# A Fourier transform and soft-routed expert kernel on one core: a new written order for the first phase's 404 steps, and seven PSUM banks of one kind

## The chip, the cores and the metric

The kernel runs on one core of one Trainium2 chip. Its time is device time in microseconds (us), from launch to end. It was timed three times before the change: 188.17, 188.81 and 190.61 us, so the median is 188.81 us. The engines are PE (TensorE matmuls; PEld is its weight loads), DVE (VectorE), ACT (ScalarE), POOL (GpSimd) and SP, which here only issues DMAs.

## The reference

```python
X = np.fft.fft(x, axis=1); X = np.fft.fft(X, axis=2)      # x: (8, 2496, 256)
x = X.real.reshape(8 * 2496, 256)
logits = x @ phi                                           # phi: (256, 32)
d = np.exp(logits - logits.max(0)); d /= d.sum(0) + 1e-9   # over all 19968 rows
slot_input = (d.T @ x).reshape(8, 4, 256)
slot_out[e] = np.maximum(slot_input[e] @ w1[e], 0) @ w2[e] # 8 experts, w1 256x1024, w2 1024x256
c = np.exp(logits - logits.max(1)); c /= c.sum(1) + 1e-9   # over the 32 slots
return c @ slot_out.reshape(32, 256)                       # (19968, 256)
```

All of it is float32.

## The kernel before

The eight sequences are handled as four pairs p = 0 to 3. Each pair's rows come in five tiles x (p, t), 1 MB each, with every row next to its mirror row. The transform is never formed in full: it is pushed through phi and through the sums.

**Phase one** is a chain of small steps per pair, named by a letter code, a pair and one or two indices:

- `f`, `g` (lines 254 and 260, DVE): add the second batch row of a tile to the first, then form the even part and the odd part in `eo`. `g` has two steps for each tile, and after both the tile's buffer is free.
- `pt`, `et` (lines 289 and 295): PE transposes `eo` into a PSUM bank, and ACT copies it out. For pair 3 the host already supplies the tile turned round as well (`xT`), so its `h` and `et` (lines 275 and 279) are DVE sums with no PE work, and the plain tiles of pair 3 come later, for `f` and `g` alone.
- `z`, `zs`, `zt`, `ztc`, `a`, `ac`, `lp`, `lm`, `lc`, `l0`, `l1` (lines 310 to 410): matmuls, transposes and copies that end in the logits of the pair, in halves.
- `mx`, `mt`, `ml`, `me`, `mu`, `nm`, `ex`, `dp` (lines 416 to 458): the maximum over a group of rows, its way through PE and back (`me` spreads it with its sign turned, `nm` copies it out of PSUM), the exponential on ACT, and sums and differences of it on DVE.
- `e`, `ec`, `d`, `dc`, `tok`, `tc`, `u`, `uc` (lines 470 to 538): the transform of the weights, copied out of PSUM, and the weighted sum of `eo`. `u` is 40 matmuls, eight for each of the pair's five `eo` tiles.

Each step is a closure, and the list PLAN says in which order they are recorded. PE, DVE and ACT keep that order exactly. An engine waits at a step whose input is not there, with everything behind it.

**Between the phases** (from line 585): `part_m` joins the four pairs, makes the slot inputs `sT`; `part_l` multiplies by w1 (line 644), applies the relu on ACT (652), and transposes on DVE (656); `part_v` multiplies by w2 into the tile `so` (664); `part_r` spreads the result into `rh` (679 to 681).

**Phase two** takes the softmax over the slots (`logits`, `less_max`, `exp`, `over_sum`: cT, cm and c, lines 696 to 723), transposes it (lT, line 757), multiplies by `rh` (po, 779), copies each bank out on ACT or DVE (787) and writes 20.4 MB (792). ORDER lists its parts.

**Loads.** SP issues all of them, in one order. A load waits for its buffer: there are six buffers of 1 MB for x and xT (`ring`), and 15 of 512 KB for `eo`. The weights reuse them. The load w1_0 takes the buffer of the last xT tile, after its two `et` steps; w1_1 to w1_5 take the buffers of pair 3's plain tiles, each after its two `g` steps; w1_6, w1_7 (in halves) and the first w2 piece take pair 1's `eo` after `u1`; the next five w2 pieces pair 2's after `u2`, then five pair 3's after `u3`; the last three wait until `part_l` has read w1 pieces. w1 and w2 are 8.4 MB each. A load that waits holds up all loads behind it.

**PSUM** has eight banks of 512 columns: two of the kind p1 (for pt, z and, later, cT and lT), five of the kind pp (for all else) and one for `u` and `so`. After line 681 the pp banks and the last one become six po banks.

Of the kernel before, what the change touches and what calls it, by code (L numbers as in the profile page):

```python
# [17 lines left out]
GS = 3  # L18
# [12 lines left out]
DE = 2  # L31
FIRST = [0, 1]
GATE = {0: ['u', 'acc', 'acc'], 1: ['rep', 'rep', 'rep']}
P1, P2 = 2, 5
W2 = [1, 1, 1, 1, 1, 1, 1, 1, 1, 1, 1, 2, 2, 1]
PLAN = (
# [97 lines left out]
def _build(nc, tc, xh, xth, phih, w1h, w2h, cins, where, out):  # L134
# [4 lines left out]
    with ctx:  # L139
        cp = ctx.enter_context(tc.tile_pool(name="cp", bufs=1))  # L140
        sb = ctx.enter_context(tc.tile_pool(name="sb", bufs=1))
        p1 = ctx.enter_context(tc.tile_pool(name="p1", bufs=P1, space=PSUM))
# [3 lines left out]
        pool_o = []  # L146
# [19 lines left out]
        def bank1(name, dt=F32):  # L166
            return p1.tile([128, 512], dt, name=name, tag="p1")
# [78 lines left out]
        def x_steps(p, t):  # L246
# [15 lines left out]
            def dest(k):  # L262
                if qi == 0:
                    tr[p, u, k] = et([128, 4, 2, nq, NA], f"et{p}_{u}_{k}")
                return tr[p, u, k][:, :, :, qi]
# [19 lines left out]
            def turn(k):  # L285
                b = held["pt", p, t, k] = bank1(f"pt{p}_{t}_{k}")
                dest(k)
# [50 lines left out]
        def a_steps(p, b):  # L338
# [36 lines left out]
            def _():  # L375
                if b == 0:
                    o1[p] = sa([120, 2, NG, NA], f"o1{p}")
# [496 lines left out]
```

## Time and profile before

| what | us |
| --- | --- |
| median of three timed runs | 188.81 (188.17 to 190.61) |
| the profiled execution, whole | 187.61 |
| its span, first to last instruction | 185.8 |
| PE, DVE, ACT, POOL busy in the span | 159.2, 133.4, 103.3, 20.9 |
| bytes moved | 64.27 MB, 346 GB/s over the span |

The profile is of one execution. A busy PE is not a PE at its peak, because matmuls are pipelined and their ends are modelled; so the rows of PE are read by when one group starts after another. The chain of waits follows the work that ended last back to the start.

### The profile page before, as it was taken

The page shows a single profiled execution, that of the slowest core. Times are in us where ns is not written, and L with a number is a line of the kernel's source. Part 1 is how long each engine was busy: PE and PEld are TensorE (multiplying, and loading weights), DVE is VectorE, ACT ScalarE, POOL GpSimd, SP SyncE. Part 2 cuts the span into 40 slices and gives each one's busy share as a digit, 9 for nine tenths or more (in the row PEclk, how much of TensorE's full clock was granted, in tenths as well). Part 3 has the DMA queues.
Part 4 walks back from the last instruction along what each step waited for, and adds up shares of the span by engine and source line. Part 5 has one row for each costly group of instructions (what it writes and reads, how often), then busy time and mean ns, then how long its engine had stood idle before and what let it go on. Part 6 is the DMA issues. An engine that isn't in the chain of part 4 may idle for free.

```text
span 185.8 us, 4196 instructions
## 1 busy us (share of the span) xinstructions
PE 159.2 (86%) x1674; PEld 101.1 (54%) x1674; DVE 133.4 (72%) x243; ACT 103.3 (56%) x232; POOL 20.9 (11%) x25
## 2 busy tenths in 40 slices
PE   0399858999999999999999999966967998989920
PEld 0384448678757587559759773533534454364410
DVE  0599869959998999999994366700595986892630
ACT  2035563659679486459458434402777797753620
POOL 0000000000000000000000006400055522540000
PEclk9999996999999999999999999999999999955975
DMA  5999999999973099745999999991399999998896
GB/s 167 410 427 414 421 418 418 425 415 424 418 253 164 4 356 363 296 146 185 407 411 356 412 410 406 421 409 70 118 403 412 389 402 424 417 416 351 370 423 284
DMA packets 11394, 64.27 MB, mean 346 GB/s; under 512 B 1392, under 2 KB 1776, under 8 KB 6128
## 3 DMA queue, kind: packets, MB, share of 16 engines
q1 hardware_dynamic: 11376, 64.02, 86.2%
q8 instruction: 13, 0.21, 0.5%
q14 instruction: 5, 0.04, 0.1%
HBM read 43.57 MB, written 20.45 MB: 344 GB/s over the span
## 4 chain that ended last, share of the span: by engine, by line
PE 61%; DMA 25%; DVE 3%; ACT 3%; issue 1%; POOL 1%; SPq 1%; DVEq 0%; ACTq 0%
PE po L779 16%; DMA w<-w2h 13%; DMA x<-xh 12%; PE a L366 6%; PE z L310 6%; PE e L470 5%; PE d L492 5%; PE pt L289 5%; PE u L527 4%; PE lT L757 3%; PE lm L395 3%; PE lp L395 3%; PE zt L349 2%; ACT o L787 1%; DVE x L254 1%
## 5 line engine op out<-in xcount | busy, mean ns | idle before, releaser
L779 PE MATMUL po<-lTs,rh 32*128 32x512 f32 (+2 forms) x192 | 34.0, 617 | 2.5 <-ACT lTs L760 2.5
L787 DVE COPY o<-po 128x512 f32<-128x512 f32 (+1 forms) x40 | 25.1, 665 | 11.7 <-PE po L779 11.6
L254 DVE TENSOR_TENSOR x<-x 128x1024 f32<-128x1024 f32 (+1 forms) x20 | 23.3, 1165 | 9.6 <-DMA x<-xh 9.6
L289 PE MATMUL pt<-cs,eo 128*128 128x128 f32 x120 | 20.2, 308 | 10.5 <-DVE eo L260 10.3
L295 ACT COPY et<-pt 128x512 f32<-128x512 f32 x30 | 17.3, 594 | 19.0 <-PE pt L289 18.7
L787 ACT COPY o<-po 128x512 f32<-128x512 f32 (+1 forms) x40 | 21.3, 581 | 9.7 <-PE po L779 9.3
L260 DVE TENSOR_TENSOR eo<-x 128x512 f32<-128x512 f32 x40 | 25.7, 684 | 0.4
L289 PEld LDWEIGHTS pt<-cs,eo 128*128 128x128 f32 x120 | 15.4, 158 | 15.4 <-DVE eo L260 7.7
L779 PEld LDWEIGHTS po<-lTs,rh 32*128 32x128 f32 x192 | 14.7, 209 | 14.0 <-ACT lTs L760 5.9
L310 PE MATMUL z<-et,wphi 128*32 128x256 f32 (+1 forms) x288 | 17.5, 363 | 0.8 <-ACT et L295 0.7
L713 POOL TENSOR_TENSOR c<-c,cm 128x640 f32<-128x640 f32 x8 | 10.0, 1263 | 64.4 <-DVE cm L712 64.4
L451 ACT ACTIVATE d<-lt,nm 120x128 f32<-120x128 f32 x44 | 13.7, 392 | 0.2 <-DVE nm L444 0.2
L366 PE MATMUL a<-cs,zt 128*120 128x128 f32 x88 | 12.3, 292 | 0.0
L366 PEld LDWEIGHTS a<-cs,zt 128*120 128x120 f32 x88 | 11.0, 196 | 1.4 <-issue 1.4
L723 POOL TENSOR_TENSOR c<-c,cm 128x640 f32<-128x640 f32 x8 | 10.1, 1264 | 11.6 <-DVE cm L722 11.1
L310 PEld LDWEIGHTS z<-et,wphi 128*32 128x32 f32 x288 | 7.4, 112 | 7.1 <-ACT et L295 2.0
L492 PE MATMUL d<-e,cs 128*64 128x320 f32 x64 | 11.1, 448 | 0.0
L470 PE MATMUL e<-cs,dpm 120*64 120x120 f32 x176 | 10.4, 269 | 0.0
L527 PE MATMUL u<-eo,ds 128*32 128x129 f32 x320 | 10.3, 274 | 0.0
L664 PE MATMUL so<-w,hT 128*32 128x256 f32 x128 | 7.7, 381 | 3.0 <-DMA w<-w2h 3.0
L470 PEld LDWEIGHTS e<-cs,dpm 120*64 120x64 f32 x176 | 9.1, 137 | 1.9 <-issue 0.4
L716 ACT ACTIVATE c<-c 128x640 f32<-128x640 f32 x8 | 5.9, 739 | 6.5 <-POOL c L713 6.5
(90 smaller groups left out, 214.5 us busy)
## 6 DMA issues: line engine op xcount, KB each, us to landing
x<-xh SPq DMA_DIRECT2D x16, 1024.0 KB, 12.0
out<-o SPq DMA_DIRECT2D x13, 1024.0 KB, 5.3
w<-w1h SPq DMA_DIRECT2D x6, 1024.0 KB, 7.3
w<-w2h SPq DMA_DIRECT2D x12, 512.0 KB, 11.2
xT<-xth SPq DMA_DIRECT2D x4, 1024.0 KB, 10.5
x<-xh SPq DMA_DIRECT2D x4, 896.0 KB, 9.4
out<-o SPq DMA_DIRECT2D x4, 896.0 KB, 6.0
out<-o SPq DMA_DIRECT2D x5, 512.0 KB, 3.7
```

Source lines behind the costliest of these rows:

```text
L254: v.tensor_tensor(x[:, first:4], x[:, first:4], x[:, 4 : 8 - first], op=ALU.add)
L260: v.tensor_tensor(eo[p, t][:, :, 128 * k : 128 * k + 128], lo, hi, op=(ALU.add, ALU.subtract)[k])
L289: pe.transpose(b[:, g * 128 : g * 128 + 128], eo[p, t][:, g, k * 128 : k * 128 + 128], ident)
L295: sc.copy(tr[p, u, k][:, :, :, qi], b.rearrange("p (g h a) -> p g h a", g=4, h=2))
L310: pe.matmul(z[32 * g : 32 * g + 32, o : o + n], wphi[:, w, :], tr[p, u, k][:, g].rearrange("p h q a -> p (h q a)"), start=w != 0, stop=w != 1,
L366: pe.matmul(ps[:120, i * 128 : i * 128 + 128], zt[p][:, GS * g : GS * g + GS].rearrange("p s h c -> p (s h c)"), C("wa"), start=True, stop ...
L451: sc.activation(d[:, g], L()[:, g], AF.Exp, bias=nm[:, g : g + 1], scale=1.0)
L470: pe.matmul(ps[64 * k : 64 * k + 64, 120 * i : 120 * i + 120], dpm[p, hf][:, k, 3 * j + i, :], C(name), start=True, stop=True, tile_positi ...
L492: pe.matmul(ps[64 * h : 64 * h + 64, :320], C("wb")[:, 64 * k : 64 * k + 64], esb[p].rearrange("p g (s h c) -> p (g s) h c", h=2, c=NKC)[: ...
L527: last = pe.matmul(ub[32 * g : 32 * g + 32, 0:129], dsb[p][:, k, c, :], e[:, 0:129] if k == 0 else e[:, 127:256], start=cc == 0, stop=cc == 9,
L779: ins = pe.matmul(po[h][:, q * n : q * n + n], rh[0][rows, dc], lT[rows, :n], start=True, stop=True, tile_position=(32 * i, 0),)
L787: ins = ev(ot[:, at_ : at_ + w], po[h][:, :w])
```

## The change

PLAN is a different order of the same 404 steps. ORDER is the same. A list ON_V names the steps of kinds `et`, `ac`, `ec`, `dc`, `nm` and `me` that DVE does; the others of these kinds are on ACT. Before, DVE did all eight `me`, all eight `nm` and the eight `dc` of odd index. Now it does two `nm`, two `dc`, two `et` and five `ec`, eleven steps in all.

The pool p1 is opened only after line 681. Until then pt, z, cT and lT take banks of pp, which has seven. The step that makes a tile first is no longer always index 0, so tests of the kind `b == 0` become tests of whether the tile is there. In GATE the third cT of pair 0 is held until the slot inputs instead of the joined sum.

```diff
-DE = 2
-GATE = {0: ['u', 'acc', 'acc'], 1: ['rep', 'rep', 'rep']}
-P1, P2 = 2, 5
+GATE = {0: ['u', 'acc', 'slot'], 1: ['rep', 'rep', 'rep']}
+P1, P2 = 2, 7
 PLAN = (
-    "f00 g001 g000 pt001 pt000 et001 f01 psphi et000 g011 g010 pt011 f02 pt010 et011 wphi g021 z001 et010 "
...
+    "f00 g001 g000 pt001 pt000 et001 f01 psphi g011 g010 pt011 f02 et011 wphi g021 et000 z001 g020 f03 pt010 "
...
+ON_V = (
+    "et031 et100 nm30 ec211 ec210 dc200 nm31 ec301 ec310 ec311 dc310"
+).split()
...
-        p1 = ctx.enter_context(tc.tile_pool(name="p1", bufs=P1, space=PSUM))
-        pool_o = []
+        pool_o, p1 = [], []
...
-            return p1.tile([128, 512], dt, name=name, tag="p1")
+            return p1[0].tile([128, 512], dt, name=name, tag="p1") if p1 else bank(name, dt)
+
+        def move(key, dst, src):
+            (v.tensor_copy if key in ON_V else sc.copy)(dst, src)
...
-                sc.copy(tr[p, u, k][:, :, :, qi], b.rearrange("p (g h a) -> p g h a", g=4, h=2))
+                move(f"et{p}{t}{k}", dest(k), b.rearrange("p (g h a) -> p g h a", g=4, h=2))
...
-                v.tensor_scalar(mex, m.unsqueeze(2).to_broadcast([n, GS, 40]), -1.0, None, op0=ALU.mult)
+                src = m.unsqueeze(2).to_broadcast([n, GS, 40])
+                if "me" + q in ON_V:
+                    v.tensor_scalar(mex, src, -1.0, None, op0=ALU.mult)
+                else:
+                    sc.mul(mex, src, -1.0)
...
-                v.tensor_copy(nm, held.pop(("mt", q))[:120, 128 : 128 + n])
+                move("nm" + q, nm, held.pop(("mt", q))[:120, 128 : 128 + n])
...
-                    sc.copy(esb[p][:, a0 : a0 + w, :].rearrange("p g n -> p (g n)"), ps[:, : 120 * w])
+                    move(f"ec{q}{j}", esb[p][:, a0 : a0 + w, :].rearrange("p g n -> p (g n)"), ps[:, : 120 * w])
...
-                    (v.tensor_copy if DE >> k & 1 else sc.copy)(dst, ps[:, :320].rearrange("p (s c) -> p c s", c=NKC))
+                    move(f"dc{q}{k}", dst, ps[:, :320].rearrange("p (s c) -> p c s", c=NKC))
...
             banks.close()
+            p1.append(ctx.enter_context(tc.tile_pool(name="p1", bufs=P1, space=PSUM)))
```

**Place one: DVE ahead of the loads w1_1 to w1_4.** In these names `eo3_1<-x3_1` is a `g` step of pair 3, tile 1; `x3_0<-x3_0` is its `f`; `dpm` is `dp`, `lt` is `l1` or `l0`, `mex` is `me`. Before:

```order
L444 COPY nm2_0_1011<-mt2_0_964 120x6
L254 TENSOR_TENSOR x3_0_125<-x3_0_125 128x768
L502 COPY ds1_947<-d1_1_1_1008 128x20x16
L444 COPY nm2_1_1035<-mt2_1_975 120x5
L260 TENSOR_TENSOR eo3_0_1037<-x3_0_125 128x4x128 x2
L457 TENSOR_TENSOR dpm2_0_1052<-d2_0_1017 120x384
L458 TENSOR_TENSOR dpm2_0_1052<-d2_0_1017 120x384
L260 TENSOR_TENSOR eo3_1_1098<-x3_1_127 128x4x128 x2
L260 TENSOR_TENSOR eo3_2_1107<-x3_2_129 128x4x128 x2
```

And now:

```order
L264 TENSOR_TENSOR eo3_1_965<-x3_1_124 128x4x128
L419 TENSOR_REDUCE mx2_1_975<-lt2_736 120x5
L264 TENSOR_TENSOR eo3_1_965<-x3_1_124 128x4x128
L264 TENSOR_TENSOR eo3_3_993<-x3_3_128 128x4x128
L430 TENSOR_REDUCE mall_99<-mt2_1_987 5x3
L464 TENSOR_TENSOR dpm1_1_1001<-d1_1_958 120x320
L465 TENSOR_TENSOR dpm1_1_1001<-d1_1_958 120x320
L264 TENSOR_TENSOR eo3_4_1012<-x3_4_130 128x4x128
L409 TENSOR_TENSOR lt3_1006<-lt3_1006,lm3_0_999 120x6x64
L264 TENSOR_TENSOR eo3_4_1012<-x3_4_130 128x4x128
```

Tile 0 of pair 3 was first and is now last of the five; the first load in this series waits for tile 1, the second for tile 4, then 3, 2 and 0. The `nm` and `dc` of pairs 1 and 2 are gone from this engine's row.

**Place two: PE around the arrival of tile (1, 2).** `pt1_2_1` needs that tile, `a0_0` only pair 0. Before:

```order
L349 MATMUL zt0_2_320<-cs0_70,zs0_215 128x128 x2
L289 MATMUL pt1_2_1_325<-cs0_70,eo1_2_311 128x128 x4
L289 MATMUL pt1_1_0_333<-cs0_70,eo1_1_273 128x128 x4
L366 MATMUL a0_0_340<-cs2_72,zt0_266 120x128 x4
L289 MATMUL pt1_2_0_346<-cs0_70,eo1_2_311 128x128 x4
L310 MATMUL z1_0_356<-et1_0_1_288,wphi_100 32x256 x8
```

And now:

```order
L369 MATMUL a0_2_319<-cs2_69,zt0_283 120x128 x3
L369 MATMUL a0_1_323<-cs2_69,zt0_283 120x128 x4
L369 MATMUL a0_0_329<-cs2_69,zt0_283 120x128 x4
L292 MATMUL pt1_1_0_337<-cs0_67,eo1_1_299 128x128 x4
L398 MATMUL lp0_1_345<-o10_334,cs2_69 120x320
L398 MATMUL lm0_1_349<-o10_334,cs2_69 120x320
L292 MATMUL pt1_2_0_352<-cs0_67,eo1_2_342 128x128 x4
```

The three `a` of pair 0 and half of its `lp` and `lm` now stand ahead of the first transpose that needs tile (1, 2).

**Place three: DVE after the slot inputs.** `cm0` and `c0` are pair 0's softmax, `hT` the transposed hidden layer. Before:

```order
L626 COPY sT_1370<-slotin1_1441 128x32
L712 TENSOR_REDUCE cm0_0_1494<-c0_1476 128x20
L712 TENSOR_REDUCE cm0_1_1502<-c0_1476 128x20
L720 TENSOR_REDUCE cm0_0_1494<-c0_1476 128x20
L721 TENSOR_SCALAR cm0_0_1494<-cm0_0_1494 128x20
L722 RECIPROCAL cm0_0_1494<-cm0_0_1494 128x20
```

And now:

```order
L633 COPY sT_1367<-slotin1_1438 128x32
L663 STREAM_TRANSPOSE hT00_1458<-hs00_1456 128x512
L663 STREAM_TRANSPOSE hT01_1471<-hs01_1469 128x512
L720 TENSOR_REDUCE cm0_0_1491<-c0_1473 128x20
L720 TENSOR_REDUCE cm0_1_1499<-c0_1473 128x20
L663 STREAM_TRANSPOSE hT10_1518<-hs10_1516 128x512
```

The hidden layer's transposes came after the whole of pair 0's softmax and now go among it.

## Rows read from the trace of the kernel before

**Rows 1.** The page's slices: GB/s moved in 40 equal slices of the span.

```profile
GB/s 167 410 427 414 421 418 418 425 415 424 418 253 164 4 356 363 296 146 185 407 411 356 412 410 406 421 409 70 118 403 412 389 402 424 417 416 351 370 423 284
```

**Rows 2.** Stretches: length, busy PE, PEld, DVE, ACT, POOL, clock, DMA share, GB/s.

```profile
28.50:40.00 11.50, 11.44 (x119) 8.82 (x120) 10.04 (x13) 6.38 (x12) 0.00 (x0) 0.85 1.01 422
80.00:97.00 17.00, 16.94 (x212) 11.26 (x210) 16.66 (x37) 10.68 (x30) 0.00 (x0) 1.00 0.80 303
132.40:185.80 53.40, 41.28 (x243) 20.87 (x241) 35.66 (x64) 31.95 (x63) 15.07 (x12) 0.84 0.94 384
```

**Rows 3.** The chain that ended last: start, length, what.

```profile
30.17 1.71 PE a L366 x8
...
33.60 0.59 PE pt L289 x4
...
34.76 1.06 PE a L366 x8
...
37.41 0.44 PE pt L289 x4
...
103.72 11.38 DMA w<-w2h
...
115.17 12.79 DMA w<-w2h
...
129.83 0.82 PE cT L696 x8
130.65 1.92 PE po L779 x12
```

**Rows 4.** Timeline of SP: start, length, issue (loads w1_1, w1_2, w1_5).

```profile
85.52 0.33 SPq L574 DMA_DIRECT2D w<-w1h  x1
...
87.66 0.33 SPq L574 DMA_DIRECT2D w<-w1h  x1
...
96.31 0.33 SPq L574 DMA_DIRECT2D w<-w1h  x1
```

**Rows 5.** What DVE waited for, 28.5 to 97.8 us: total, times, longest.

```profile
DVE lt L406 <- PE lm L395: 2.4, 2, 2.2
```

**Rows 6.** Groups by line: busy, mean ns | idle before.

```profile
L260 DVE TENSOR_TENSOR eo<-x 128x512 f32<-128x512 f32 x40 | 25.7, 684 | 0.4
...
L457 DVE TENSOR_TENSOR dpm<-d 120x384 f32<-120x384 f32 (+1 forms) x8 | 4.2, 520 | 2.2 <-ACT d L451 2.1
...
L406 DVE TENSOR_TENSOR lt<-lt,lm 120x384 f32<-120x384 f32 (+1 forms) x8 | 4.0, 517 | 2.5 <-PE lm L395 2.4
...
L502 DVE COPY ds<-d 128x320 f32<-128x320 f32 x8 | 3.9, 482 | 3.3 <-PE d L492 3.3
...
L434 DVE TENSOR_SCALAR mex<-mall 6x120 f32<-6x120 f32 (+1 forms) x8 | 2.0, 256 | 0.0
...
L444 DVE COPY nm<-mt 120x6 f32<-120x6 f32 (+1 forms) x8 | 1.2, 152 | 0.1
```

**Rows 7.** Timeline of DVE: start, length, work, and the idle time before it.

```profile
26.47 1.22 DVE L254 TENSOR_TENSOR x<-x 128x1024 f32<-128x1024 f32 x1 [1.45 <-DMA x<-xh]
...
82.72 0.94 DVE L254 TENSOR_TENSOR x<-x 128x768 f32<-128x768 f32 x1
...
100.86 0.48 DVE L458 TENSOR_TENSOR dpm<-d 120x320 f32<-120x320 f32 x1
```

**Rows 8.** Timeline of PE: start, length, work, and the idle time before it.

```profile
28.56 1.61 PE L289 MATMUL pt<-cs,eo 128*128 128x128 f32 x8 [2.56 <-DVE eo L260]
...
105.71 2.39 PE L527 MATMUL u<-eo,ds 128*32 128x129 f32 x76
...
110.98 7.10 PE L644 MATMUL h<-w,sT 128*32 128x512 f32 x64
...
117.87 4.96 PE L664 MATMUL so<-w,hT 128*32 128x256 f32 x88
...
128.00 0.64 PE L664 MATMUL so<-w,hT 128*32 128x256 f32 x8 [0.17 <-DMA w<-w2h]
```

More of the change, by code (lines that the diff above doesn't have):

```diff
@@ L262, in dest @@
             def dest(k):
-                if qi == 0:
+                if (p, u, k) not in tr:
                     tr[p, u, k] = et([128, 4, 2, nq, NA], f"et{p}_{u}_{k}")
@@ L286, in turn @@
                 b = held["pt", p, t, k] = bank1(f"pt{p}_{t}_{k}")
-                dest(k)
                 for g in range(4):
@@ L329, in _ @@
             def _():
-                if u == 0:
+                if p not in zs:
                     zs[p] = sb.tile([128, 10, 128], F32, name=f"zs{p}", tag="zs", bufs=2)
@@ L342, in _ @@
             def _():
-                if b == 0:
+                if p not in zt:
                     zt[p] = sa([128, GS * NG, 2, NKC], f"zt{p}")
@@ L375, in _ @@
             def _():
-                if b == 0:
+                if p not in o1:
                     o1[p] = sa([120, 2, NG, NA], f"o1{p}")
                 ps = held.pop(("a", p, b))
-                sc.copy(o1[p][:, :, 4 * b : 4 * b + n, :], ps[:120, : n * 128].rearrange("p (u r k) -> p r u k", u=n, r=2))
+                move(f"ac{p}{b}", o1[p][:, :, 4 * b : 4 * b + n, :], ps[:120, : n * 128].rearrange("p (u r k) -> p r u k", u=n, r=2))
         def c_steps(p, hf):
@@ L401, in _ @@
             def _():
-                if hf == 0:
+                if p not in lt:
                     lt[p] = sb.tile([120, NG, 2, NA], F32, name=f"lt{p}", tag="lt", bufs=LT)
@@ L464, in _ @@
                 def _():
-                    if hf == 0 and j == 0:
+                    if p not in esb:
                         esb[p] = se([128, NG, 120], f"e{p}")
@@ L487, in _ @@
                 def _():
-                    if hf == 0 and k == 0:
+                    if p not in dsb:
                         dsb[p] = se([128, 2, NKC, NSLOT], f"ds{p}")
```

40 rows, old and new, of the table PLAN are left out of this document.

## The prediction, made before the changed kernel ran

> **What bounds the kernel now.** I began with the slices [rows 1]. The DMA engines move about 415 GB/s for the first 51 us (the x tiles), fall to 4 GB/s in the fourteenth slice, pick up, and from about 88 us on run full again until 126 us: these are the weights. Then they rest once more, and the output fills the end, 53.4 us at a DMA share of 0.94 [rows 2]. So the questions are what starts the weights and what starts the output.
>
> The chain of waits answers the second [rows 3]. It ends phase one in two DMA pieces of w2: the last is issued at 115.17 and lands 12.79 us later, at 127.96. On PE the last eight matmuls of `so` start at 128.00, after a wait for that DMA [rows 8], and everything of phase two follows. PE had begun `so` at 117.87, so matmuls were not what was late.
>
> SP's timeline answers the first [rows 4]. The loads w1_1, w1_2 and w1_5 go out at 85.52, 87.66 and 96.31. Each is the moment at which DVE finishes the two `g` steps of one tile of pair 3. From the issue of w1_1 to the last landing are 42.4 us, from that of w1_2 40.3 us. The 15 MB in between need nearly all of that at the rate of rows 1, so the weights are late because DVE is late.
>
> And DVE is late because it is full: 16.66 of 17.0 us from 80 to 97 us, against 10.68 us for ACT [rows 2]. Between 28.5 and 97.8 us its longest single wait is 2.2 us, for `lm` [rows 5]. PE looks as full (16.94 of 17.0 us), but what gates the loads w1_1 to w1_5 stands on DVE.
>
> **DVE, the term that counts.** Prices are busy time over count [rows 6]: `g` 0.64, `me` 0.25, `nm` 0.15, `dc` 0.49, `l1` 0.50, `dp` two instructions of 0.52; the `f` of tile 0 takes 0.94 [rows 7].
> - Ahead of w1_2's last `g` there stand no longer six `me` (1.5), six `nm` (0.9), four `dc` (2.0), the `f` and both `g` of tile 0 (0.94 + 1.28) and one `dp` (1.04): 7.7 us. New there are three `g` (1.9) and one `l1` (0.5): 2.4 us. The difference is 5.3 us, and w1_2 goes at 87.66 - 5.3 = 82.4.
> - Ahead of w1_1 the same `me`, `nm`, `dc`, tile 0 and another `dp` are gone (7.7 us), and two `g` new (1.3 us): 85.52 - 6.4 = 79.1.
> - w1_5, now tile 0 and last, loses seven `me`, the six `nm` and four `dc` (4.6 us) and two steps of pair 3's `l` (1.0 us): 96.31 - 5.6 = 90.7.
> - Two `et` come to DVE, early. They stand where DVE waits for tiles of pair 1 (1.45 us before 26.47 [rows 7]), so I cost them at nothing. Without that cover they would cost 1.3 us, each taken as one `g`.
>
> All this holds if DVE waits as long as before. The bounds: with its 2.4 us wait [rows 5] gone the gates are 2.4 us earlier still; in the worst case all 5.3 us come back as waits on ACT and PE.
>
> The last w2 piece then lands at 79.1 + 42.4 = 121.5 by w1_1, or 82.4 + 40.3 = 122.7 by w1_2. I take the later, 5.3 us before 127.96. The loads after `u1`, `u2` and `u3` have a queue of more than 8 us ahead of them (10 us and more from issue to landing in the chain's w2 pieces), so they need not be issued earlier.
>
> **PE.** Fewer changes of tile shape: I count 79 changes between neighbouring steps in the old order and 54 in the new. Four transposes take 0.44 us after a step of their own shape and 0.59 us after a `z` [rows 3]; 25 changes at 0.15 us are 3.8 us. The `a`, `lp` and `lm` put into the wait before 28.56 (2.56 us [rows 8]) fill it. None of this moves a gate on DVE, so it adds nothing to the end; it buys slack for `so`. `so` cannot end before `u3`'s end plus 9.8 us (108.10 to 117.87) plus its own 7.2 us (128 records at the rate of 88 in 4.96 [rows 8]). DVE's last `dp` ended at 101.34 [rows 7], and `u3` 6.8 us after it. Up to that `dp` DVE loses eight `me`, six `nm`, six `dc` (5.8 us) and gains two `ec`, priced as `dc`, and one `dc` (1.5 us): it ends at 97.0, `u3` at 103.8, and `so` could end at 120.8. The weights at 122.7 + 0.6 are later, with 2.5 us between.
>
> **ACT** takes what DVE gave. It has 6.3 idle us in 17 [rows 2], which covers it.
>
> **PSUM.** Until line 681 one kind of bank serves all. After it, the reopened p1 overlays old banks, and cT of pair 1 must wait for the copy to `rh`, which used to run beside it. The eight cT take 0.82 us [rows 3] and stand ahead of `po`. Between 0 and 0.82 I take 0.5 us, since part of that copy is waited for anyway.
>
> **The sum**, against the profiled execution: 187.61 - 5.3 + 0.5 = 182.8 us. The median of the timed runs, 188.81, lies 1.2 us above that execution; I add a third of this and forecast **183.2 us**.
>
> **A rule against the change.** The copies out of PSUM go from a shared arrangement mostly to ACT, and rows 2 show why that can pay: DVE is busy for 98% of the stretch that gates the loads and ACT for 63%. The Trainium skill, TensorEngine Tiling (Array Packing), section PSUM Bottleneck, says that after tiling the copies may become the bottleneck and that both ScalarE and VectorE should make them. By that rule the `nm` and `dc` would have stayed on DVE. The sum without them would be 2.9 us smaller in its gain, 186.1 us. I go by the rows.
>
> **Rivals.**
> 1. *DVE waits less.* PE runs ahead and the 2.4 us wait for `lm` goes: 183.2 - 2.4 = 180.8 us. For it: place two of the change and 25 fewer shape changes put PE ahead. Against it: `me` and `nm` now hop over ACT, so the chain of a maximum is longer. Chance 0.14.
> 2. *No gain: the work off DVE comes back as waits.* `dp` needs `ex`, which needs `nm`, `mu`, `me` on ACT and PE by turns. The point is 5.3 us of added waits ahead of w1_2. Then the end is 187.61 + 0.5 + 0.4 = 188.5 us. Rows 5 speak against (DVE hardly waits), the narrower spacing of these steps for. Chance 0.20.
> 3. *The clock.* PE waited 2.56 us before 28.56, and in the stretch after it the granted clock averaged 0.85; eight records of `a` took 1.71 us there and 1.06 us later, which is 1.2 GHz against 2.4 GHz. If PE now waits for DVE in more places, this recurs. The mean of 0.85 over 11.5 us is 3.4 us at half speed, 1.7 us lost; three such stretches lose 5 us, `u3` ends at 108.9, `so` at 125.9, and the whole is 187.61 - 2.7 + 0.9 = 185.8 us. The Trainium skill, TensorE: Matmul & The Clock Gate, section HAM oscillation, says that waits between bursts of matmuls throw the clock back to half each time; one fall in this trace agrees. Chance 0.05.
> 4. *Slower: banks held by DVE.* With one kind of bank, `d` of pair 0, `a` of pair 3 and others now take banks that `lm` holds until DVE's `l0`. PE then waits for DVE with all behind it. `so` decides from the point where `u3` ends after 111.6 (128.64 less 17.0). Five such waits of 2.4 us, the one known size [rows 5], put `u3` at 115.8 and `so` at 132.8: 187.61 + 4.2 + 0.9 = 192.7 us. Against it: these waits also shrink when DVE has less to do. Chance 0.06.
>
> That the change does not do what it says is half true: its shape changes save PE time that the end does not need.
>
> **Chances.** My forecast has 0.55, with a range of its own from 181.4 to 185.4 us (queue and landing, and the bounds of the cT wait). Two per cent of 188.81 us is 3.8 us, about what a measurement here can tell; so faster means under 185.0 us. Rival 1 and nine tenths of the forecast lie there: 0.64. Rivals 2 and 3 and the rest are within 2%: 0.30. Slower: 0.06. The range that holds eight in ten goes from rival 1, with 0.8 us for its own spread, to rival 2: 180.0 to 188.6 us.
>
> **What would show it.** In the changed profile: w1_1 issued near 79, w1_2 near 82, w1_5 near 91; the last w2 piece landing near 122.7 and `so` ending right after; DVE's busy share ahead of the gates still over 0.95; `u3` ending near 104. If w1_2 goes after 86, rival 2 holds. If `so` ends more than 1 us after the last landing, PE is the bound, and rivals 3 or 4 are to be looked for. If the output stretch differs from 53.4 us by over 1.5 us, the last assumption, that phase two only shifts, was wrong.

## The result, and the profile after

The changed kernel took 181.11 us, the median of four runs (180.25 to 182.08), beside 188.9 us for the kernel before. The ratio is 0.958, with a 95% interval of 0.950 to 0.966. On another chip, where the kernel before took only 186.12 us, the same kernel came to 0.976 (0.968 to 0.984). So it is faster, by 4.2% on the one chip and 2.4% on the other. Executions of one kernel fall into faster and slower ones here, so every ratio compares the faster ones alone, and it can differ from that of two medians. The prediction was 183.2 us, in a range of 180.0 to 188.6.

The profiled execution took 181.24 us, its span 179.5 us: 6.4 us less than the one before. Its slices, first the granted clock of TensorE in tenths, then GB/s [rows 1]:

```profile
PEclk9999999999999999999999969999999999855975
GB/s 165 394 422 428 407 420 422 418 422 413 425 408 381 327 418 354 7 228 349 369 365 414 409 409 411 420 154 0 320 406 408 384 413 415 418 414 354 360 429 247
```

The weights start earlier, and one slice at about 105 us has a clock of 0.6 that was not there before. SP's timeline shows how much earlier: w1_1, w1_2 and w1_5 against [rows 4].

```profile
76.68 0.33 SPq L581 DMA_DIRECT2D w<-w1h  x1
...
79.94 0.33 SPq L581 DMA_DIRECT2D w<-w1h  x1
...
87.13 0.82 SPq L581 DMA_DIRECT2D w<-w1h  x1
```

They go out 8.8, 7.7 and 9.2 us earlier, where 6.4, 5.3 and 5.6 were forecast. The last w2 piece lands at 120.20 instead of 127.96.

Now what DVE waited for, from about 27 us to behind these loads (total, times, longest), first after, then the same view of the kernel before up to its w1_2:

```profile
DVE x L258 <- DMA x<-xh: 0.7, 1, 0.7
```

```profile
DVE lt L406 <- PE lm L395: 2.2, 1, 2.2
DVE x L254 <- DMA x<-xh: 1.8, 2, 1.5
DVE dpm L457 <- ACT d L451: 0.5, 1, 0.5
```

The waits for PE and ACT are gone. The stretches say the same of both engines at once. The columns are those of rows 2. The first pair of lines goes from one and the same step, the `f` of tile (1, 2), to the issue of w1_2; the second from the start of the span to the end of `u3`. The kernel before, then the changed one:

```profile
26.47:87.66 61.19, 59.10 (x696) 42.20 (x700) 57.66 (x99) 40.81 (x105) 0.40 (x3) 0.97 0.77 299
27.09:79.94 52.85, 52.75 (x621) 39.26 (x621) 52.78 (x82) 40.20 (x108) 0.40 (x3) 1.00 0.88 352
```

```profile
0.00:108.11 108.11, 96.77 (x1193) 69.08 (x1194) 89.01 (x161) 63.18 (x155) 0.79 (x9) 0.98 0.86 336
0.00:101.25 101.25, 92.18 (x1192) 70.01 (x1192) 86.75 (x147) 62.36 (x168) 0.79 (x9) 1.00 0.92 363
```

Up to w1_2, DVE has 4.9 us less work, and its 3.5 idle us are gone as well. But look at PE, the first number behind the length. In the first pair it was busy for 59.10 of 61.19 us and is busy for 52.75 of 52.85. The way to `u3`'s end became 6.9 us shorter because PE's own time did: it is busy for 4.6 us less and stands still for 2.3 us less.

Part of this belongs to the one execution that was profiled before the change. Its tile (1, 2) landed at 26.45, PE stood still for it for 2.56 us [rows 8], and then the granted clock fell. The same stretch of that kernel, and of a run below that has the same order and the same banks, but whose tile landed at 25.64:

```profile
28.50:34.00 5.50, 5.44 (x40) 4.63 (x40) 5.43 (x8) 2.35 (x4) 0.00 (x0) 0.69 1.01 420
28.50:34.00 5.50, 5.50 (x57) 3.96 (x56) 5.29 (x8) 3.56 (x7) 0.00 (x0) 1.00 0.99 411
```

In the changed kernel the tile landed later still, at 27.06, and neither happened: PE had the `a`, `lp` and `lm` of place two to do.

Behind `u3` the gain shrinks again. PE's timeline from there, against [rows 8]:

```profile
98.86 2.39 PE L534 MATMUL u<-eo,ds 128*32 128x129 f32 x76
101.80 0.43 PE L622 MATMUL accT<-cs,acc 128*128 128x64 f32 x2 [0.55 <-DVE acc L620]
102.16 0.22 PE L623 MATMUL accT<-cs,acc 128*1 128x32 f32 x2
102.70 0.63 PE L630 MATMUL slotin<-at,cs 128*128 128x32 f32 x4 [0.32 <-DVE at L625]
103.17 0.61 PE L631 MATMUL slotin<-at,cs 128*128 128x32 f32 x4
103.84 3.38 PE L651 MATMUL h<-w,sT 128*32 128x512 f32 x16
107.15 1.33 PE L704 MATMUL cT<-cs,lt 120*128 120x120 f32 x9
108.40 1.93 PE L651 MATMUL h<-w,sT 128*32 128x512 f32 x16
110.26 0.42 PE L704 MATMUL cT<-cs,lt 120*128 120x120 f32 x2
110.61 3.64 PE L651 MATMUL h<-w,sT 128*32 128x512 f32 x32
114.07 7.09 PE L671 MATMUL so<-w,hT 128*32 128x256 f32 x128
121.09 0.66 PE L765 MATMUL lT<-cs,c 128*128 128x128 f32 x4
121.65 0.70 PE L686 MATMUL sorep<-sos,cs 128*128 128x256 f32 x2
122.96 1.01 PE L704 MATMUL cT<-cs,lt 120*128 120x120 f32 x8 [0.61 <-DVE rh L688]
123.90 1.99 PE L787 MATMUL po<-lTs,rh 32*128 32x512 f32 x12
```

From `u3`'s end (101.25) to the start of `so` PE needs 12.8 us, not 9.8: eleven transposes cT of pair 0 now stand between the h matmuls, where they used to fill `part_m`'s pauses (four of them from 108.04 and seven from 109.16), and the first 16 h take 3.38 us and the next 16 take 1.93 (the clock of 0.6). `so` then runs through without a wait, ends at 121.16, and `po` starts 2.74 us later instead of 1.94. The stretch from the first output on is as before [rows 2]:

```profile
125.67:179.40 53.73, 41.28 (x243) 20.88 (x241) 35.48 (x64) 31.93 (x63) 15.07 (x12) 0.84 0.93 381
```

### The profile page after: what moved, and what is told of

It reads as the page before. It is cut to its first block, busy times and chain, and to the rows that moved or that the text cites. A ratio compares the mean times of both kernels' runs of the same rounds, so it can differ in the third digit from the quotient of the medians.

```text
span 179.5 us, 4195 instructions
## 1 busy us (share of the span) xinstructions
PE 156.4 (87%) x1674; PEld 101.9 (57%) x1674; DVE 130.7 (73%) x230; ACT 102.2 (57%) x245; POOL 20.8 (12%) x25
## 4 chain that ended last, share of the span: by engine, by line
PE 79%; DVE 4%; DMA 4%; ACT 4%; issue 2%; POOL 1%; SPq 1%; DVEq 0%; ACTq 0%; POOLq 0%
PE po L787 15%; PE pt L292 9%; PE z L313 9%; PE a L369 6%; PE e L477 6%; PE h L651 5%; PE d L499 5%; DMA phi<-phih 4%; PE u L534 4%; PE so L671 4%; PE lT L765 3%; PE lm L398 3%; PE lp L398 3%; PE zt L352 3%; PE cT L704 2%
## 5 line engine op out<-in xcount | busy, mean ns | idle before, releaser
L171 ACT COPY et<-pt 128x512 f32<-128x512 f32 x28 | 15.5, 594 | 19.3 <-PE pt L292 19.3
L292 PE MATMUL pt<-cs,eo 128*128 128x128 f32 x120 | 19.1, 308 | 7.6 <-DVE eo L264 7.5
L313 PE MATMUL z<-et,wphi 128*32 128x256 f32 (+1 forms) x288 | 15.9, 361 | 0.7 <-ACT et L171 0.7
L313 PEld LDWEIGHTS z<-et,wphi 128*32 128x32 f32 x288 | 8.2, 112 | 6.4 <-ACT et L171 2.1
L369 PE MATMUL a<-cs,zt 128*120 128x128 f32 x88 | 11.3, 278 | 0.0
L709 ACT COPY c<-cT 128x480 f32<-128x480 f32 (+1 forms) x12 | 5.9, 528 | 9.5 <-PE cT L704 9.5
L369 PEld LDWEIGHTS a<-cs,zt 128*120 128x120 f32 x88 | 10.3, 183 | 1.0 <-ACT zt L360 0.6
L477 PE MATMUL e<-cs,dpm 120*64 120x120 f32 x176 | 10.9, 270 | 0.0
L499 PE MATMUL d<-e,cs 128*64 128x320 f32 x64 | 9.5, 434 | 0.0
L704 PEld LDWEIGHTS cT<-cs,lt 120*128 120x128 f32 x44 | 4.7, 146 | 8.1 <-issue 3.3
```

What stands on the lines that cost most here:

```text
L171: (v.tensor_copy if key in ON_V else sc.copy)(dst, src)
L292: pe.transpose(b[:, g * 128 : g * 128 + 128], eo[p, t][:, g, k * 128 : k * 128 + 128], ident)
L313: pe.matmul(z[32 * g : 32 * g + 32, o : o + n], wphi[:, w, :], tr[p, u, k][:, g].rearrange("p h q a -> p (h q a)"), start=w != 0, stop=w != 1,
L369: pe.matmul(ps[:120, i * 128 : i * 128 + 128], zt[p][:, GS * g : GS * g + GS].rearrange("p s h c -> p (s h c)"), C("wa"), start=True, stop ...
L477: pe.matmul(ps[64 * k : 64 * k + 64, 120 * i : 120 * i + 120], dpm[p, hf][:, k, 3 * j + i, :], C(name), start=True, stop=True, tile_positi ...
L499: pe.matmul(ps[64 * h : 64 * h + 64, :320], C("wb")[:, 64 * k : 64 * k + 64], esb[p].rearrange("p g (s h c) -> p (g s) h c", h=2, c=NKC)[: ...
```

## The experiments

The theories at the start. **A**, the prediction's: DVE's work ahead of the loads sets the loads, and they set the end. **B**, which the stretches suggest: PE is as full as DVE, and its time in phase one, with its changes of tile shape, is what shrank. The stretches below are cut as above: from the `f` of tile (1, 2) to w1_2's issue, or from the start to `u3`'s end.

### The old split of copies in the new order

```diff
-    "et031 et100 nm30 ec211 ec210 dc200 nm31 ec301 ec310 ec311 dc310"
+    "me00 me01 me10 me11 me20 me21 me30 me31 nm00 nm01 nm10 nm11 nm20 nm21 nm30 nm31 dc001 dc011 dc101 dc111 dc201 dc211 dc301 dc311"
```

> The changed kernel with its order and its banks, but with the old split of copies: DVE again does all eight me, all eight nm and the eight dc of odd index, and none of the ec, et or other dc. My theory: the loads of the weights are set by how much work stands ahead of them on DVE. Ahead of w1_2's last g six me (1.5 us), six nm (0.9) and four dc (2.0) come back, 4.4 us. So w1_2, issued at 79.94 in the changed kernel, goes near 84.3, the last w2 piece lands near 124.6 instead of 120.20, so ends near 125.3, and the whole takes 185 us (184 to 186). The rival, that the order alone (tile 0 last, steps of pair 3 elsewhere) moved the loads: w1_2 stays within 1 us of 79.94 and the whole within 1 us of 181.1.

Measured: 184.47 us, ratio to the kernel before 0.978 (0.970 to 0.986), the profiled execution 182.31 us. The time is near what A said, the steps are not. w1_2 went at 81.14, 1.2 us later and not 4.4, and the last piece landed at 120.95:

```profile
26.03:81.14 55.11, 53.64 (x631) 39.63 (x631) 55.04 (x95) 37.87 (x95) 0.40 (x3) 1.00 0.86 348
0.00:104.11 104.11, 92.72 (x1192) 68.91 (x1192) 88.16 (x160) 61.14 (x155) 0.79 (x9) 1.00 0.90 359
```

In the new order six `me` and five `nm`, but only two of the `dc`, stand ahead of w1_2, and 2.3 us of DVE work come back there (52.78 to 55.04). By busy time over count they would be 3.2 us. But a DVE step can start before the one ahead of it has ended; in the kernel before, an `nm` starts at 82.66 and the step behind it at 82.72 [rows 7], 0.06 us later:

```profile
82.66 0.14 DVE L444 COPY nm<-mt 120x6 f32<-120x6 f32 x1
```

Read this way, from one start to the next, a `me` takes 0.19 us and a `dc` 0.40, and the sum is 2.2 us. So the prices of small steps in the prediction are too high.

DVE is full, so all of it shows: the stretch is 2.3 us longer. It began 1.1 us earlier, because tile (1, 2) landed earlier in this execution, and so w1_2 is 1.2 us late. `u3` ends 2.9 us later. PE's busy time has hardly changed (92.72 against 92.18) and it stands still for 2.3 us more; its largest two waits are for `mex` (DVE, 1.3 us) and `e` (ACT, 1.4 us). So the split is worth about 2.9 us at `u3` once the new order is there.

### The new split in the old order

```diff
+ON_V = (
+    "et031 et100 nm30 ec211 ec210 dc200 nm31 ec301 ec310 ec311 dc310"
+).split()
```

> The kernel before with its order, its banks and its GATE, but with the new split of copies. My theory: the split alone takes 4.4 us (six me, six nm, four dc) from DVE ahead of w1_2: its issue moves from 87.66 to about 83.3, the last landing from 127.96 to about 123.6, the whole to 183 to 185 us. The rival, that it is the order that lets DVE go ahead, and that in the old order the steps now on ACT come back as waits: w1_2 after 86 and the whole 187 to 189 us.

Measured: 187.65 us, ratio 0.988 (0.977 to 0.999). w1_2 at 85.81, the last landing at 126.04, `u3`'s end at 108.31, where it was 108.11. DVE has 2.2 us less to do up to w1_2, and PE is full:

```profile
25.66:85.81 60.15, 60.08 (x716) 42.37 (x719) 55.42 (x85) 45.61 (x124) 0.39 (x3) 1.00 0.81 321
```

PE is busy for 60.08 of 60.15 us and DVE now idles for 4.7. The stretch is 1.0 us shorter than in the kernel before; the other 0.8 us by which w1_2 is earlier are the earlier landing of tile (1, 2). More than half of the work taken off DVE came back as waits, the largest three for `dp`, 2.5 us together. That is the prediction's rival 2 at work, and it speaks for B.

### Seven banks of one kind, order and split as before

```diff
-P1, P2 = 2, 5
+P1, P2 = 2, 7
```

> The kernel before with its order, its split and its GATE, but with seven PSUM banks of one kind until the spreading of the slot outputs. My theory: the banks are no part of the gain. Phase one stays within 1 us (w1_2 near 87.7), cT of pair 1 now waits for the copy to rh, and the whole is the same as before up to 0.8 us later: 187.6 to 189.5 us. The rival, that the shared banks are what let PE run ahead and DVE wait less: w1_2 before 85.5 and the whole under 186. A second rival, that banks held by DVE stop PE: the whole over 191.

Measured: 188.49 us, ratio 1.000 (0.995 to 1.006), the same. But not step by step: w1_2 went at 85.06 and `u3` ended at 105.50, 2.6 us earlier both. The wait for `lm` is gone, and the clock of 0.85 with it:

```profile
0.00:105.50 105.50, 95.48 (x1192) 67.95 (x1192) 88.78 (x160) 62.68 (x155) 0.79 (x9) 1.00 0.87 344
```

That this is the work of the banks is not shown. Tile (1, 2) landed at 24.85 here, 1.6 us earlier than in the profile before. The run with the new split above has the old banks and an early tile, and there the clock stayed at 1.00 and the wait for `lm` was 0.4 us instead of 2.2. The clock alone is 1.7 us of PE time, as worked out from [rows 2] in rival 3.

The whole gained nothing: cT of pair 0 moved between the h (`u3`'s end to `so` 11.2 us, not 9.8), the last landing came 1.6 us earlier only, `po` started 2.7 us after `so`, and the output took 55.1 us in this execution.

### Split and banks together, and tile 0 last

The first of these two kernels has the new split and banks and the old order:

> The kernel before with its order and its GATE, but with both the new split of copies and the seven banks of one kind. Alone the split moved w1_2 from 87.66 to 85.81 (less work on DVE, but new waits) and the banks to 85.06 (the 2.14 us wait for lm gone). My theory: the two add, because with the banks the steps that went to ACT and PE no longer come back as waits: w1_2 near 83, the last landing near 123.5, the whole 184 to 186 us by its first to last instruction plus 1.8; the new order then gives the other 3 to 4 us. The rival, that the order is what makes both pay: w1_2 at 85 or later and the whole 187 us or more.

Measured: 187.6 us, ratio 0.9950 (0.9895 to 1.0005); w1_2 at 85.47, `u3`'s end at 107.97. The two did not add, so the rival was right: the order makes them pay.

```profile
0.00:107.97 107.97, 94.62 (x1192) 67.18 (x1192) 87.90 (x147) 64.41 (x168) 0.79 (x9) 1.00 0.88 346
```

With the run before it and the old split in the new order, this gives all four pairings of order and split under the same seven banks, each with the clock at 1.00 up to `u3`. The one word of GATE goes with the order here; below it moves no cT. PE's time without work counts from the start of the span:

| order, split | PE busy, us | PE without work, us | `u3` ends | ratio |
| --- | --- | --- | --- | --- |
| old, old | 95.48 | 10.02 | 105.50 | 1.000 |
| old, new | 94.62 | 13.35 | 107.97 | 0.995 |
| new, old | 92.72 | 11.39 | 104.11 | 0.978 |
| new, new | 92.18 | 9.07 | 101.25 | 0.958 and 0.976 |

The order takes 2.8 us off PE's busy time with the old split and 2.4 with the new one. The split acts on the waits: in the old order it adds 3.3 us of them, in the new one it removes 2.3. These are single profiles; in six profiles with the new split in the new order (one step moved in two of them), `u3` ended between 100.77 and 101.73. The new order with the old banks was not run.

The second adds one part of the order:

```diff
-    "me20 ztc31 f34 d101 zs32 mu20 d110 dc101 zt32 me21 dc110 d111 nm20 f30 ztc32 mu21 ex20 tok1 a30 dc111 "
-    "nm21 g301 a31 g300 tc1 ac30 a32 dp20 ac31 u1 ac32 g311 ex21 g310 g321 g320 lp30 uc1 dp21 lp31 lc30 g331 "
+    "me20 ztc31 f34 d101 zs32 mu20 d110 dc101 zt32 me21 dc110 d111 nm20 ztc32 mu21 ex20 tok1 a30 dc111 "
+    "nm21 a31 tc1 ac30 a32 dp20 ac31 u1 ac32 g311 ex21 g310 g321 g320 lp30 uc1 dp21 lp31 lc30 g331 "
...
-    "ml30 g341 mt31 d201 dc200 me30 ml31 d210 g340 mu30 dc201 d211 dc210 me31 nm30 tok2 ex30 mu31 dc211 nm31 "
+    "ml30 g341 f30 g300 g301 mt31 d201 dc200 me30 ml31 d210 g340 mu30 dc201 d211 dc210 me31 nm30 tok2 ex30 mu31 dc211 nm31 "
```

> The kernel before with the new split, the seven banks, and of the new order one part alone: f30, g300 and g301, the sums of pair 3's tile 0 (0.94 + 1.28 = 2.2 us of DVE, the largest single term of the prediction's sum), go behind g341, the last of the other tiles. Beside it stands the same kernel without that move (w1_2 at 85.47, u3's end 107.97, last landing 125.21, so's end 126.24). The prediction's reasoning: 2.2 us less DVE work ahead of w1_1 to w1_4, so w1_2 goes at 83.3, the last landing is at 123.0, and the whole falls by 2.2 us. My theory now: phase one is as long as PE's own work with its changes of tile shape, so u3's end stays at 107.5 to 108.5, so still ends 18.3 us after it, and though the loads go out 2 us earlier the whole stays within 0.7 us of that kernel (about 187 us).

Measured: 191.98 us, ratio to the kernel before 1.031 (1.019 to 1.042), slower. Both theories missed. One half step of the other tiles, g340, still stands behind the moved ones. DVE's timeline around the place, first without the move, then with it:

```profile
78.73 2.07 DVE L238 TENSOR_TENSOR x<-x 128x1024 f32<-128x1024 f32 x2
80.83 1.29 DVE L244 TENSOR_TENSOR eo<-x 128x512 f32<-128x512 f32 x2
83.21 0.56 DVE L444 TENSOR_TENSOR dpm<-d 120x384 f32<-120x384 f32 x1 [1.08 <-ACT d L438]
```

```profile
78.19 1.20 DVE L238 TENSOR_TENSOR x<-x 128x1024 f32<-128x1024 f32 x1
82.70 0.56 DVE L444 TENSOR_TENSOR dpm<-d 120x384 f32<-120x384 f32 x1 [3.31 <-ACT d L438]
```

The 2.2 us of tile 0 had filled the wait for the exponential. With them gone DVE waits 3.31 us instead of 1.08 at the same `dp`, and the load behind tile 1 goes only 0.5 us earlier, at 84.96. Later the moved steps delay `dc` of pair 2 and `dp` of pair 3: PE waits 1.4 us ahead of `tok` and 1.9 ahead of `u`, where it had waited 1.5 ahead of `u` alone. Behind these waits the granted clock fell (0.50 from 100 to 102 us), and the 76 `u` that follow took 3.84 us instead of 2.39. So `u3` ends 3.3 us later, and about 1.6 of them are the clock. In the full new order three `g` and an `l1` have come ahead of the gates for it.

### PE's shape changes put back

In the changed kernel and, apart, in the kernel before:

```diff
                 b = held["pt", p, t, k] = bank1(f"pt{p}_{t}_{k}")
+                if p in (1, 2):
+                    pe.matmul(b[:32, 0:1], wphi[:, 0, :], ident[:, 0:1], start=True, stop=True, tile_position=(0, 0))
```

> The changed kernel with one extra matmul of a single column and 128x32 weights ahead of each of the 20 pt groups of pairs 1 and 2, into the bank that the transposes then overwrite. By count the 54 changes of tile shape between neighbouring steps become 87. At 0.15 us for a change and some 0.1 us for each extra matmul this is 5.0 + 2.0 = 7 us of PE. My theory: in the changed kernel PE sets the end of phase one (u3 ends near 101.2, and so follows from it), so most of it arrives at the end: +4 to +7 us, 185 to 188 us. The rival, that PE has slack or that a change of shape costs nothing: under +1 us, 181 to 182.

Measured in the changed kernel: 187.34 to 191.66 us. The mean of its faster executions is 187.4 us, that of the kernel before on the same chip 187.7: the gain is gone.

```profile
26.44:84.38 57.94, 57.94 (x665) 42.58 (x665) 53.04 (x83) 40.69 (x109) 0.40 (x3) 1.00 0.82 326
0.00:106.89 106.89, 97.21 (x1232) 73.21 (x1232) 86.91 (x148) 62.73 (x168) 0.79 (x9) 1.00 0.88 347
```

DVE's work and its order are untouched (53.04 us against 52.78), and yet w1_2 goes 4.4 us later. What DVE waited for up to 99 us:

```profile
DVE et L283 <- PE z L315: 1.9, 1, 1.9
DVE lt L411 <- ACT lt L409: 1.7, 1, 1.7
DVE dpm L466 <- ACT tok L527: 1.6, 1, 1.6
DVE dpm L466 <- ACT d L460: 1.2, 1, 1.2
```

All but the third are new: steps that DVE takes from PE directly or by way of ACT. So PE's time reaches the loads though DVE's work is the same; A alone does not hold. With the old split in the new order, where DVE's added work delayed w1_2 in full, it says that in the new order either engine can set the loads.

PE's busy time up to `u3` grew by 5.0 us for 33 changes and 20 one-column matmuls. What one change costs can be read where the same steps stand in both kernels, here without and with the added matmuls (`pt<-cs,wphi`):

```profile
33.19 1.93 PE L313 MATMUL z<-et,wphi 128*32 128x256 f32 x32
35.06 1.09 PE L292 MATMUL pt<-cs,eo 128*128 128x128 f32 x8
36.08 1.73 PE L313 MATMUL z<-et,wphi 128*32 128x256 f32 x40
```

```profile
35.14 1.93 PE L315 MATMUL z<-et,wphi 128*32 128x256 f32 x32
36.89 0.20 PE L292 MATMUL pt<-cs,wphi 128*32 128x1 f32 x2
37.02 0.66 PE L294 MATMUL pt<-cs,eo 128*128 128x128 f32 x4
37.60 0.22 PE L292 MATMUL pt<-cs,wphi 128*32 128x1 f32 x2
37.76 0.66 PE L294 MATMUL pt<-cs,eo 128*128 128x128 f32 x4
38.34 1.73 PE L315 MATMUL z<-et,wphi 128*32 128x256 f32 x40
```

Behind a `z`, whose shape it shares, the added matmul costs nothing that shows: from `z` to `pt` it is 1.87 us without and 1.88 with it. Between two `pt` it makes two changes, and from the first `pt` to the next `z` it is 1.02 us without and 1.32 with it. So a change costs 0.15 us, and the matmul far less than the 0.1 us that was expected. The Trainium skill, TensorEngine Tiling (Array Packing), section Key Properties, says that changing the tiling mode drains the engine. The trace agrees in that each change has a cost, the 0.15 us above.

> The same extra matmuls in the kernel before: its 79 changes of shape become 113, again about 7 us of PE. The prediction said that PE's shape changes do not reach the end there, because the weights are later: so could have ended at 125.1 and ended at 128.64, a slack of 3.5 us. With 7 us more on PE and no effect on DVE's gates, u3 would end near 115 and the whole would be 3 to 4 us later, 191 to 192.5 us. If the added PE work also makes DVE wait (for lm and the like), the gates move with it and the whole is 194 us or more. If the changes cost nothing, it stays at 188 to 189 us.

Measured in the kernel before: 190.63 us, ratio 1.011 (1.006 to 1.017). w1_2 went 1.1 us later, `u3` ended 1.25 us later and the last piece landed 0.9 us later. PE's busy time to `u3` grew by 3.6 us only (96.77 to 100.40), because the clock, which had cost 1.7 us in the profile before, did not fall this time (tile (1, 2) landed at 25.13); PE also stood still for 2.4 us less. What was left reached the loads and the end, without waiting for a slack to be used up. How large PE's slack was the run does not show: 5.3 us of added work less the 3.5 us of slack would leave 1.8, and the time grew by 2.1.

### Behind phase one

The step g321 moved right behind g320:

```diff
-    "lc31 g330 d100 ec111 ec110 g320 d101 dc100 dp20 d110 uc0 d111 dc110 mx30 e201 dc101 nm21 dc111 g321 e200 "
+    "lc31 g330 d100 ec111 ec110 g320 g321 d101 dc100 dp20 d110 uc0 d111 dc110 mx30 e201 dc101 nm21 dc111 e200 "
```

> The changed kernel with one step moved: g321, the last g of the tile for w1_4, right behind g320 instead of ten DVE steps later. w1_4 was issued at 84.01 in the changed kernel, 3 us after w1_3. If the weights still set the end, w1_4 goes near 82.2, the last w2 piece lands up to 1.5 us earlier, near 118.9, and the whole falls by as much, to 179.8. My theory is that the bound has moved: so, which ended 0.96 us after the last landing, is now set by u3 and what PE does behind it, so the landing moves and the whole does not: 180.6 to 181.4 us.

Measured: 181.28 us, ratio 0.964 (0.958 to 0.970). w1_4 went at 81.40, the last piece landed at 119.02, 1.2 us earlier; `so` ended at 120.81, 0.35 us earlier, by just as much as `u3`. So the weights no longer set the end.

The other three ran beside the changed kernel itself:

> The changed kernel once more, as it is, so that the other kernels of this call have it on the same chip beside them. 181.1 us, within 1 us.

Measured: 183.16 us (180.67 to 184.53), ratio 0.976.

```diff
-GATE = {0: ['u', 'acc', 'slot'], 1: ['rep', 'rep', 'rep']}
+GATE = {0: ['u', 'acc', 'acc'], 1: ['rep', 'rep', 'rep']}
```

> The changed kernel with one word of GATE put back: the third cT of pair 0 may run after the joined sum (acc) and not only after the slot inputs. My theory: with these transposes between accT and slotin PE does not pause in part_m, the clock stays at its full level in the slice where it was 0.6 of it, and from u3's end to so's start take the 9.8 us of the kernel before and not 12.8. so then starts 2 to 3 us earlier, but ends no earlier than the weights let it (120.20 + 0.64 = 120.84 against 121.16), so the whole falls by 0.3 us only: 180.4 to 181.2. The rival, that the changed h stretch has nothing to do with GATE: so's start stays at 114.1 and h's first 16 records at 3.4 us.

Measured: 181.35 us, ratio 0.973 (0.966 to 0.980). The rival was right: no cT moved, h's first 16 took 3.58 us. The kernel with the new banks and the old GATE had its cT between the h as well, and all three kernels with the old banks had them in `part_m`. So it is the shared banks that put them there.

```diff
-    "w00 m00 l00 s00 l10 v00 v10 k00 r00 x10 o00 k01 g01 x16 h01 g02 x17 h02 x12 x13 k02 g03 x14 h03 x15 x20 "
+    "w00 m00 l00 s00 l10 v00 v10 k00 r00 o00 x10 k01 g01 x16 h01 g02 x17 h02 x12 x13 k02 g03 x14 h03 x15 x20 "
```

> The changed kernel with the first output part of pair 0 ahead of cT of pair 1 in the order (o00 before x10). In the changed kernel cT waits for the copy to rh and po stands behind it: 2.81 us from so's end to po. My theory: po starts 0.8 to 1.0 us earlier, right after rh, the first output goes out as much earlier, and since the output stretch is bound by the DMA queues the whole falls by as much, to 180.2. The rival: cT of pair 1, and with it the softmax of pair 1, is late instead, the stretch from the first output to the end grows by as much, and the whole stays at 181.

Measured: 182.29 us, ratio 0.977 (0.971 to 0.983). `po` came 1.80 us after `so`, 0.9 us closer, and the first output went out at 124.31. The output then took 56.3 us, so the rival's account fits.

> The changed kernel with three edits together: g321 right behind g320, the word of GATE put back, and o00 ahead of x10. My theory: alone each runs into the other's bound, together they add. The last w2 piece lands near 119.0 (as with g321 alone), PE is ready for so well before, so ends near 119.7 (1.5 us earlier than in the changed kernel), po follows 0.8 to 1.0 us closer, and the whole falls by 2.3 us to 178.8 (178.3 to 179.5). The rival, that PE still sets so's end or that the output stretch gives it back: 180 us or more.

Measured: 183.17 us, ratio 0.984 (0.978 to 0.989). `so` ended at 119.96, right behind the last landing at 119.28, and the first output went out at 123.50, 2.2 us earlier. The output took 57.1 us instead of 53.8 and gave back more than that. The same 8 us of it, with the three edits and in the changed kernel:

```profile
131.00:139.00 8.00, 6.38 (x38) 3.67 (x39) 4.13 (x10) 5.07 (x11) 2.53 (x2) 0.62 0.78 316
```

```profile
131.00:139.00 8.00, 5.61 (x51) 3.28 (x49) 6.01 (x13) 6.21 (x14) 2.98 (x3) 1.00 1.02 410
```

The clock fell early and the DMA queues ran short. Whether the edit to ORDER makes the clock fall there or the later softmax of pair 1 does it without the clock isn't settled. No version tried beats the changed kernel by more than the runs scatter.

## Why the prediction was right, and where it was not

The time lies 2.1 us under the forecast and in the wide range, but just outside the forecast's own range (181.4 to 185.4 us): it is at rival 1 (180.8 us), which had a chance of 0.14. So the number came out while the path to it was in part another.

**DVE, the term that counts.** The work term was nearly right. From the `f` of tile (1, 2), 26.47 before [rows 7] and 27.09 after, to w1_2 it is 61.19 us before and 52.85 after, 8.3 us less; 4.9 of them are work (57.66 to 52.78), where 5.3 were forecast, and 3.5 are waits that vanished, the largest for `lm` (2.2 us). That `f` started 0.6 us later, so w1_2 went 7.7 us earlier. The two `et` were free, as forecast: DVE still waited 0.70 us for the tile behind them, whose load had gone out at 12.36 instead of 11.77. In a second execution, below, the tile had landed by then and they were not. For w1_5 the count left out one `mx` (0.81 us) and one `ml` (0.26).

**The step that failed** is "All this holds if DVE waits as long as before", and behind it the one on PE: "None of this moves a gate on DVE, so it adds nothing to the end; it buys slack". PE was nearly full in the kernel before (59.10 of 61.19 us up to w1_2), and then what one engine saves or loses shows in the waits of the other. The runs with the old order show it from one side: 2.2 us off DVE shortened the way to w1_2 by 1.0 us and did not move `u3`, and under the seven banks `u3` even came 2.5 us later. The run with extra shape changes shows it from the other: 5.0 us more on PE moved the loads by 4.4 us and `u3` by 5.6. I had seen that PE was busy for 16.94 of 17 us [rows 2] and set it aside because the gates stand on DVE.

**Its size was about right, though.** 25 changes at 0.15 us were forecast as 3.8 us. The price holds. PE's busy time to `u3` fell by 4.6 us, 2.9 without the clock's 1.7; against the old order with the new banks, where the clock did not fall either, it fell by 3.3 us. That the shape changes are all of it is argued from the price: no run took them alone out of the old order. The other 2.3 us of the 6.9 are time without work. And since a late tile stopped PE in the profile before, 6.9 us says too much for the change: against the old order with an early tile and the new banks (105.50) it is 4.3 us.

**The landing** followed the gates: 7.8 us earlier where w1_2 went 7.7 earlier, so the 40.3 us from that issue held.

**`so`.** The forecast had the weights 2.5 us behind PE. In fact PE came last: `u3` ended at 101.25, not 103.8, but 12.8 us and not 9.8 lie behind it. 1.4 us of that are the cT among the h (11.2 us in the kernels with these banks where the clock stayed up), the other 1.6 the clock. `so` ended 0.96 us after the last landing, close to the point of 1 us that the prediction named.

**Phase two.** The wait of cT and `po` was forecast at 0.5 us between 0 and 0.82, and is 0.8 (2.74 less 1.94). The output stretch changed by 0.4 us. So the sum as it came is 187.61 - 7.5 (end of `so`) + 0.8 + 0.4 = 181.3 us.

**The rivals.** Rival 1 had the right place (the wait for `lm`) with 2.4 us; all waits that vanished are 3.5. Part of that is the profile it was read from, since the wait for `lm` is 0.4 us where the tile came early. Rival 2 is what the split does without the order. Rival 3, the clock, came the other way round: phase one got back its 1.7 us, and the h behind `part_m` lost 1.6. Rival 4, banks held by DVE, did not show: with the banks alone the waits became fewer.

The Trainium skill, TensorEngine Tiling (Array Packing), section PSUM Bottleneck, says to use both ScalarE and VectorE for the copies out of PSUM. The measurement goes both ways: with seven banks the split that leaves `nm` and `dc` on DVE ends `u3` 2.5 us earlier in the old order and 2.9 us later in the new one.

## What to carry to other kernels

When two engines are both nearly full in a stretch (here 94% and 97% of it), price the change on each of them over the whole stretch; in these runs work taken off one alone came back as waits, and it paid once the other had less to do too. A step that seems to stand in the way may be filling a wait, as the 2.2 us of tile 0 did. Before a wait in a single profile becomes a term of a forecast, ask whether it belongs to the kernel or to that execution, as with the late tile here. And when a bound moves by several us, look at what was 2 or 3 us behind it, since it is the next bound.

## What the runs showed of the chip that I had not expected

The granted clock changes places between executions of one kernel. In `part_m`, with the same two PE pauses of about 0.55 and 0.32 us, it fell in four of eleven profiled executions with the shared banks and stayed up in seven. A fall cost 1.6 us in each of the four: from `u3`'s end to `so` they took 12.8 us, the seven 11.2. In the output stretch it falls in every execution. Where that came after 150 us, the stretch took 53.4 to 53.8 us. Where a fall came earlier, the stretch took 54.7 to 57.1 us. Which of the two is the cause is not shown. The changed kernel shows both: at 152 to 162 us in its first profile, with a DMA share of 1.01, and in the second, the execution of 184.53 us, ten us earlier:

```profile
142.00:152.00 10.00, 9.07 (x50) 5.02 (x49) 5.76 (x12) 6.05 (x12) 2.90 (x3) 0.66 0.84 349
```

Its first output went out only 0.5 us later than in the first profile, and its span ended 3.3 us later. That this is also what scatters the runs without a trace is likely, but not shown.
